# Low parts of twelve weight units made by TensorE and ScalarE in the bank that VectorE wrote, with the planner's numbers anew

## The chip, the cores and the metric

The kernel runs on one core of one Trainium2 chip. The metric is the device time of one execution in microseconds (us). An execution was timed three times before the change: 676.77, 675.38 and 676.64 us, median 676.64 us.

## What is computed

An attention over 4 batches of 8 heads, 576 tokens and 64 dimensions (causal, with a bias from a running sum of `s`), then two feed-forward layers over the 2304 tokens. Cut to what matters:

```
scores = q @ k^T / 8 ; causal ; + min(-(cum_i - cum_j), 0)      # cum = cumsum(max(s, 0))
attn   = exp(scores - max) / (sum + 1e-9) ; x = attn @ v         # (2304, 512)
h  = x @ w_in                                                    # 512 -> 1024
sm = softmax(h) ; solu = h * sm ; ln = normalise(solu) * g_ln
x  = ln @ w_out                                                  # 1024 -> 512
h  = max(x @ w1, x @ w2, x @ w3)                                 # 512 -> 768
out = h @ w_out2                                                 # 768 -> 512
```

Each product is made to nearly 32 bits out of three fp16 products: both operands are split into a high part (fp16 of the scaled value) and a low part (fp16 of what the high part leaves), and high by high, high by low and low by high are added up.

## The kernel before, in words

**Tiles and groups.** Tokens go through in 18 tiles of 128: per pair of batches eight full tiles and one of the two 64-token tails. A tile's attention is `sc` (scores on TensorE, L788 and L794), a masked minimum on VectorE (L825, L858), the exponential on ScalarE (L877), a split of its result into high and low part, a transposition, and `av` (the product with the values, L942, L948, L961). For tiles 0 to 3 transpositions are made by TensorE in `turned` (L474); for all others by a DMA transpose (`et<-es`, tails also `ett<-est`). Then comes the first layer `m1` (L1034) with its softmax and normalisation (L1048 to L1096), and, for groups of two tiles, `m2` (L1131), `m3` (three products for the maximum, L1170, combined by L1189) and `m4` (L1204).

**Weights.** They arrive as 64-bit floats and are decoded on the chip in 40 units of 128 x 512 by `load_w`: a DMA into one of four stages (L594), three VectorE instructions that put the 32-bit value together (`dec1` L608, `dec2` L612, `dec3` L615, the last two into a bank of PSUM), `wh` on ScalarE, which writes the scaled high part (L620), and `wl` on VectorE, which writes scale times value minus high part (L622). Units 0 to 7 are `w_in`, 8 to 15 `w_out` (their scale is a column of `g_ln`), 16 to 33 `w1`, `w2`, `w3`, and 34 to 39 `w_out2`.

**Banks.** The bank of a unit is one of the three of the pool `acc`, which `turned`, `m2`, `m3` and `m4` take theirs from too. Scores, values and `h` have banks of their own.

**A low part by TensorE.** `turned` does already what the change will do for weights: after ScalarE or VectorE has written the high part, a matmul with a diagonal of -1/scale (`MINUS`, made at L532) adds minus the high part to the bank (L488), and a copy moves scale times the rest out (L491 or L492).

**Order.** No loop sets the order of instructions. `build` makes a list of operations, each with a position `pos` worked out from the table `P`, the engines that may take it and an estimate of its time; `Schedule.run` plays them through with a clock of its own, gives each engine among those that can start soon the one of lowest position, and issues everything in the order found. On the chip each engine then takes its instructions strictly in that order. A DMA counts in this plan as landed `LAT_DMA` ns after its share of the queue is over:

```
    LAT_SAME, LAT_CROSS, LAT_DMA, LAT_ISSUE = 130, 180, 1250, 650
```

Tiles of `et` (four buffers), `es` (two), `r` (three) and the three `acc` banks bound how far one engine may run ahead of another.

Of the kernel before, what the change touches and what calls it, by code (L numbers as in the profile page):

```python
# [18 lines left out]
QK_S = 16.0  # L19
# [14 lines left out]
    la=8.4,  # L34
    lp=-1.469,
    lu=-13.333,
    lv=-0.647,
    o1=-3.616,
    o2=-4.09,
    o3=-0.398,  # L40
    o4=0.334,
    ds=1.887,
    wi=-20.819,
    wid=2.708,
    wo=-15.551,
    wod=-18.167,
    w3=6.958,
    w3d=1.141,
    w4=-16.623,
    w4d=15.675,  # L50
    mp=-1.93,
    look=[2.7, 0.0, 35.7, 169.7, 69.9],
    spare=[1764.9, 1665.2, 1871.5, 968.8, -1500.0, 3960.7, 27.5],
# [6 lines left out]
    lc=-23.89,  # L60
# [35 lines left out]
class Schedule:  # L96
# [5 lines left out]
    def __init__(self, look, spare, off, eng):  # L102
        self.ops, self.last, self.readers = [], {}, {}
        self.look = dict(zip(("PE", "DVE", "ACT", "POOL", "SP"), look))

        self.spare = [dict(zip(("DVE", "ACT", "POOL"), spare[i:i + 3])) for i in (0, 3)]
        self.spare_until = spare[6]
        self.off, self.eng = off, eng
        self.unit, self.tile = "", ""

# [34 lines left out]
    def run(self):  # L145
# [114 lines left out]
        for _ in self.ops:  # L260
# [67 lines left out]
def pe(k, n):  # L328
    return k * (n / 2.4 + 2.3)
# [22 lines left out]
def build(nc, T, X, dims):  # L352
# [17 lines left out]
    S_ = Schedule(P["look"], P["spare"], P["off"], P["eng"])  # L370

# [91 lines left out]
    SCALES = (QK_S, -QK_S, E_S, 1.0)  # L463
    MINUS = lambda c: T["k_tail"][:, 2 + SCALES.index(c)]

    def turned(n, src, out, scale, r, w, pos, k):
# [11 lines left out]
        op([("PE", pe(n, 256) + 20, f)], r + ["ktail"], [ps], pos, kind=k + "p")  # L478
# [7 lines left out]
        if by_pe:  # L486
# [11 lines left out]
           [ps] + w[0], w[1], pos, kind="P" + k)  # L498

# [10 lines left out]
    def prologue():  # L510
# [8 lines left out]
        if any(P["pt"]):  # L519

            def ident():
                nc.gpsimd.memset(IDENT(), 1.0)
                for s in (1, -1):
                    nc.gpsimd.affine_select(
                        out=IDENT(), in_=IDENT(), pattern=[[-s, 128]], base=0, channel_multiplier=s,
                        compare_op=ALU.is_ge, fill=0.0,
                    )
            op([("POOL", 900, ident)], [], ["ktail"], p0 - 1, kind="ident")

            def minus():  # L530
# [55 lines left out]
    def load_w(src, hi, lo, scale, pos, wkey, extra=()):  # L586
# [17 lines left out]
        pb = buf("acc")  # L604
        f32 = lambda: pb().rearrange("p (b n) -> p b n", b=8)
        i32 = lambda: pb().bitcast(I32).rearrange("p (b n) -> p b n", b=8)
        def dec1():
# [3 lines left out]
        op([("DVE", dve1(512), dec1)], sk, [tb], pos, kind="dec1")  # L611
        op([("DVE", dve2(512), lambda: nc.vector.scalar_tensor_tensor(  # L612
            out=i32(), in0=low(), scalar=29, in1=t(), op0=ALU.logical_shift_right, op1=ALU.bitwise_or))],
           sk + [tb], [pb], pos, kind="dec2")
# [6 lines left out]
           [pb] + list(extra), [(wkey, 0)], pos, kind="wh")  # L621
        op([("DVE", dve2(512) + px * 0.57, lambda: nc.vector.scalar_tensor_tensor(  # L622
# [529 lines left out]
    def m3(g, f0):  # L1152
# [11 lines left out]
        for w in range(3):  # L1164
            ps, first = buf("acc"), ([], [])
            for f in (f0, f0 + 1):
                for kk in range(KD):
# [6 lines left out]
                    o = op([("PE", pe(3, GN), fn)], [(xk[0], 0, kk), (xk[1], 1, kk), (("w3", f, w), 0), (("w3", f, w), 1)],  # L1174
# [192 lines left out]
```

## Time and profile before

| | |
|---|---|
| median of three runs | 676.64 us |
| profiled execution, its time | 676.31 us |
| its span, first to last instruction | 674.6 us |
| TensorE busy | 621.2 us (92%) |
| VectorE busy | 464.3 us (69%) |
| ScalarE busy | 301.8 us (45%) |
| mean granted TensorE clock | 0.994 |

The span is the trace's own; 1.7 us of the profiled execution's time lie around it. Shares of busy time are means over a program with different stretches: weights are decoded in the first quarter, attention runs to about 460 us, and from there TensorE works through the second layers alone.

### The profile page before, as it was taken

The numbers are of one execution on the slowest core, as the hardware profiler recorded it, in microseconds if no ns is written. First come the engines' busy times: TensorE is split into PE (matmuls) and PEld (weight loads), VectorE is DVE, ScalarE is ACT, GpSimd is POOL, SyncE is SP. The second block draws the span as 40 slices with busy tenths as digits, with TensorE's granted clock in tenths as the row PEclk, the third lists the DMA queues.
The fourth block names the chain that finished last, engine by engine and source line by source line (L and its number), as shares of the span: only waits on it lengthen the run. The fifth ranks groups of instructions, "written<-read, shape, count | busy, mean of one in ns | idle before, by whom it ended". The sixth has DMA issues, their size and how long they took to land.

```text
span 674.6 us, 15275 instructions
## 1 busy us (share of the span) xinstructions
PE 621.2 (92%) x6188; PEld 442.7 (66%) x6188; DVE 464.3 (69%) x1109; ACT 301.8 (45%) x713; POOL 34.1 (5%) x49
## 2 busy tenths in 40 slices
PE   1579888899999999899999999989999999999997
PEld 1334556777576666667666675659767867878774
DVE  7899999997799678798888988775155245212121
ACT  3678875554476445667556546351023022110110
POOL 1101000010001101020000201000000000000000
PEclk9998999999999999999999999989999999999999
DMA  6976755569989879699999896864032022000001
GB/s 176 276 216 176 171 153 162 172 144 186 170 167 176 155 142 150 131 186 189 162 181 174 152 181 119 127 99 84 1 63 63 1 48 48 1 32 2 17 17 32
DMA packets 249351, 82.68 MB, mean 123 GB/s; under 512 B 225472, under 2 KB 244096, under 8 KB 249280
## 3 DMA queue, kind: packets, MB, share of 16 engines
q1 hardware_dynamic: 249280, 81.70, 60.0%
q8 instruction: 48, 0.79, 0.5%
q14 instruction: 23, 0.19, 0.1%
HBM read 35.95 MB, written 4.83 MB: 60 GB/s over the span
## 4 chain that ended last, share of the span: by engine, by line
PE 63%; DVE 15%; DMA 14%; issue 3%; ACT 3%; SPq 1%; POOL 0%; DVEq 0%; POOLq 0%; ACTq 0%
PE acc L1170 23%; PE acc L1131 11%; PE acc L1204 9%; PE h L1034 8%; DMA et<-es 7%; PE sc L794 4%; PE av L961 3%; PE sc L788 2%; DVE acc L612 2%; DVE acc L615 2%; DVE r L825 1%; DMA kt<-in_moe_w_in_dram 1%; DMA vs<-in_moe_w_in_dram 1%; DVE f L608 1%; DMA lnt<-ln 1%
## 5 line engine op out<-in xcount | busy, mean ns | idle before, releaser
L1170 PE MATMUL acc<-x2A,w_h 128*128 128x256 f16 x1296 | 215.5, 273 | 2.3 <-DVE f L1189 1.5
L1170 PEld LDWEIGHTS <-w_h 128*128 128x128 f16 x1944 | 187.3, 98 | 32.6 <-issue 7.6
L1170 PE MATMUL acc<-x2B,w_h 128*128 128x256 f16 x648 | 176.7, 273 | 0.0
L877 ACT ACTIVATE r<-r,mn 128x128 f32<-128x128 f32 (+4 forms) x144 | 83.0, 578 | 55.0 <-DVE mn L825 39.7
L1034 PE MATMUL h<-w_in_h,xt 128*128 128x512 f16 x432 | 101.3, 380 | 0.0
L1131 PE MATMUL acc<-lnt,w_out_h 128*128 128x256 f16 x864 | 98.2, 273 | 1.1 <-DMA lnt<-ln 1.0
L1131 PEld LDWEIGHTS <-w_out_h 128*128 128x128 f16 x864 | 83.4, 98 | 13.3 <-issue 3.3
L1189 DVE TENSOR_TENSOR f<-f,acc 128x512 f32<-128x512 f32 x54 | 36.9, 684 | 69.8 <-PE acc L1170 69.8
L1034 PEld LDWEIGHTS <-xt 128*128 128x128 f16 x432 | 40.0, 98 | 45.7 <-issue 3.6
L454 ACT ACTIVATE f<-acc 128x512 f32<-128x512 f32 x37 | 22.0, 595 | 98.5 <-PE acc L1170 57.9
L1204 PE MATMUL acc<-w2o_h,h2A 128*128 128x512 f16 x216 | 64.4, 380 | 0.0
L825 DVE CUSTOM_DVE_ANT_0 r<-sc,mask 128x128 f32<-128x128 f32 (+3 forms) x128 | 58.7, 485 | 7.1 <-PE sc L794 5.5
L434 DVE SCALAR_TENSOR_TENSOR es<-r,es 128x512 f16<-128x512 f32 (+1 forms) x89 | 56.7, 642 | 2.3 <-ACT es L405 1.7
L794 PE MATMUL sc<-kt,qt 64*128 64x256 f16 (+2 forms) x768 | 47.9, 264 | 0.7 <-DMA kt<-st 0.4
L961 PE MATMUL av<-vs,et 128*128 128x64 f16 x960 | 38.1, 195 | 5.1 <-DMA et<-es 4.8
L961 PEld LDWEIGHTS <-et 128*128 128x128 f16 x960 | 34.9, 99 | 12.0 <-DMA et<-es 7.7
L405 ACT ACTIVATE es<-r 128x512 f16<-128x512 f32 (+1 forms) x48 | 28.0, 584 | 29.4 <-DMA et<-es 25.5
L1204 PE MATMUL acc<-w2o_h,h2B 128*128 128x512 f16 x108 | 41.0, 379 | 0.0
L1055 ACT ACTIVATE ln<-e,st 128x1024 f32<-128x1024 f32 x18 | 20.7, 1150 | 42.4 <-DVE e L1048 35.7
L788 PE MATMUL sc<-ckr,cqr 6*128 6x128 bf16 (+5 forms) x192 | 28.6, 308 | 11.9 <-DMA cqr<-cum_d 9.8
L794 PEld LDWEIGHTS <-qt 64*128 64x128 f16 (+1 forms) x864 | 26.8, 99 | 18.3 <-issue 11.2
L454 ACT ACTIVATE x2A<-acc 128x512 f16<-128x512 f32 x16 | 9.5, 593 | 64.0 <-PE acc L1131 64.0
(138 smaller groups left out, 721.3 us busy)
## 6 DMA issues: line engine op xcount, KB each, us to landing
kt<-in_moe_w_dram SPq DMA_DIRECT2D x18, 256.0 KB
vs<-in_moe_w_dram SPq DMA_DIRECT2D x18, 256.0 KB
raw<-in_k_dram SPq DMA_DIRECT2D x16, 256.0 KB
raw<-in_q_dram SPq DMA_DIRECT2D x16, 256.0 KB
raw<-in_v_dram SPq DMA_DIRECT2D x16, 256.0 KB
out_dram<-f SPq DMA_DIRECT2D x16, 256.0 KB
kt<-in_moe_w_out_dram SPq DMA_DIRECT2D x7, 512.0 KB
vs<-in_moe_w_out_dram SPq DMA_DIRECT2D x7, 512.0 KB
```

The costliest lines, as they stand in the source:

```text
L434: nc.vector.scalar_tensor_tensor(out=lo(g), in0=src(g), scalar=sc1(g), in1=hi(g), op0=ALU.mult, op1=ALU.subtract)
L454: nc.scalar.activation(out=out(*a), in_=in_(*a), func=AF.Copy, scale=scale)
L788: yield lambda: nc.tensor.matmul(out=out(), lhsT=T["cqr"][cr, hp, cs], rhs=T["ckr"][cr, hp, ck], start=True, stop=False, skip_group_check= ...
L794: yield lambda n=n, qa=qa, o=o, kx=kx: nc.tensor.matmul(out=out()[:, o], lhsT=qv()[r, qa * HP + hp, ts], rhs=kx, start=False, stop=(n == 2 ...
L825: nc.vector.tensor_tensor_reduce(out=gw(R)[:, g], in0=gw(sc[y])[:, g], in1=T["mask"][:, SM - W:SM], scale=1.0 / S_MUL, scalar=3e38, op0=AL ...
L877: nc.scalar.activation(out=gw()[:, g], in_=gw()[:, g], func=AF.Exp, bias=mnf()[:, g:g + 1], scale=-1.0, accum_out=den(hs[g]),)
L961: nc.tensor.matmul(out=out, lhsT=ea_[:, ea, kb], rhs=T["v_s"][c, kb // 2][:, kb % 2, ha + a, va], start=(kb == 0 and m == 0), stop=(kb == ...
L1034: nc.tensor.matmul(out=hb()[:, n * 512:(n + 1) * 512], lhsT=xt()[:, xa, kk], rhs=T["w_in_h"][:, wa, kk, n * 512:(n + 1) * 512], start=(kk ...
L1131: nc.tensor.matmul(out=ps()[:, d % 2 * GN:(d % 2 + 1) * GN], lhsT=T["w_out_h"][:, wa, kk, d * 128:(d + 1) * 128], rhs=lnt()[:, la, kk], st ...
L1170: nc.tensor.matmul(out=ps()[:, f % 2 * GN:(f % 2 + 1) * GN], lhsT=T["w123_h"][:, w, wa, f, kk], rhs=x2(xa)[:, kk], start=(kk == 0 and i == ...
L1189: op([("DVE", dve2(2 * GN), lambda ps=ps: nc.vector.tensor_tensor(out=m(), in0=m(), in1=ps(), op=ALU.max))], pk + [m], [m], pos, kind="m3x")
L1204: nc.tensor.matmul(out=ps(), lhsT=h2(ha)[:, f, o * 128:(o + 1) * 128], rhs=T["w2o_h"][:, wa, f], start=(f == 0 and i == 0), stop=(f == KF2 ...
```

## The change

Three things. For the units 0 to 19 whose scale is a plain number, that is the eight of `w_in` and four of `w1` to `w3`, VectorE's `wl` is replaced by a matmul `wm` with the diagonal of -1/256 that takes the high part off in the bank, and by a ScalarE copy `Pw` of the rest. For this the three `acc` banks are each written once by a matmul at the start (`prime_all`), since the first value in a unit's bank comes from VectorE and the matmul has to add to it; VectorE's second decode step waits for that, and so does the first transposition. `MINUS` gets a fifth column. Second, every `m3` matmul now also waits for the low part of the odd unit of its pair. Third, 19 numbers of the table `P` and two of its lists are new (two lines shown), and `LAT_DMA` is 2087 instead of 1250 ns, so the order of nearly everything changes.

```diff
 P = dict(
-    la=8.4,
+    la=7.39,
...
+    lat=2.087,
+    wp=[0, 20, 20],
...
+    S_.LAT_DMA = int(P["lat"] * 1000)
...
-    SCALES = (QK_S, -QK_S, E_S, 1.0)
+    SCALES = (QK_S, -QK_S, E_S, 1.0, W_S)
...
-        op([("PE", pe(n, 256) + 20, f)], r + ["ktail"], [ps], pos, kind=k + "p")
+        op([("PE", pe(n, 256) + 20, f)], r + ["ktail", "prime"], [ps], pos, kind=k + "p")
...
+    def prime(bank):
+
+        nc.tensor.matmul(
+            out=bank, lhsT=MINUS(1.0), rhs=T["k_tail"].rearrange("p h t -> p (h t)")[:, 0:512], start=True, stop=True,
+        )
...
+            def prime_all():
+                for b in T["acc"]:
+                    prime(b)
+            op([("PE", 700, prime_all)], ["ktail"], ["prime"], p0 - 1, kind="prime")
...
+        by_pe = not callable(scale) and P["wp"][0] <= n_w[0] - 1 < P["wp"][1]
...
-           sk + [tb], [pb], pos, kind="dec2")
+           sk + [tb, "prime"], [pb], pos, kind="dec2")
...
+        if by_pe:
+
+            op([("PE", pe(1, 512) + 60, lambda: nc.tensor.matmul(
+                out=f32(), lhsT=MINUS(scale), rhs=hi, start=False, stop=True, skip_group_check=True))],
+               ["ktail", (wkey, 0)], [pb], pos, kind="wm")
+            op([("ACT", act(512, True), lambda: nc.scalar.activation(out=lo, in_=f32(), func=AF.Copy, scale=scale))],
+               [pb], [(wkey, 1)], pos, kind="Pw")
+            return
...
-                    o = op([("PE", pe(3, GN), fn)], [(xk[0], 0, kk), (xk[1], 1, kk), (("w3", f, w), 0), (("w3", f, w), 1)],
+                    o = op([("PE", pe(3, GN), fn)], [(xk[0], 0, kk), (xk[1], 1, kk), (("w3", f, w), 0), (("w3", f, w), 1), (("w3", f0 + 1, w), 1)],
```

Three places of the order show what moves. In the kernel after the change the lines are numbered anew: `dec1` L634, `dec2` L640, `dec3` L643, `wh` L648, `wm` L652, `Pw` L655, the transposition L485, its subtraction L499, scores L824, m2 L1167, values of a tail L978.

VectorE's queue, first weight units, before: `f` is the scratch tile of `dec1`, `kt` and `vs` are the stages, `acc` the banks.

```order
L608 TENSOR_SCALAR f_114<-kt_69 128x512
L612 SCALAR_TENSOR_TENSOR acc_131<-kt_69,f_114 128x512
L608 TENSOR_SCALAR f_115<-vs_73 128x512
L615 SCALAR_TENSOR_TENSOR acc_131<-kt_69,acc_131 128x512
L612 SCALAR_TENSOR_TENSOR acc_129<-vs_73,f_115 128x512
L615 SCALAR_TENSOR_TENSOR acc_129<-vs_73,acc_129 128x512
L622 SCALAR_TENSOR_TENSOR w_in_h<-acc_131,w_in_h 128x512
L622 SCALAR_TENSOR_TENSOR w_in_h<-acc_129,w_in_h 128x512
L608 TENSOR_SCALAR f_116<-kt_69 128x512
L612 SCALAR_TENSOR_TENSOR acc_130<-kt_69,f_116 128x512
```

The same stretch of VectorE's queue after the change:

```order
L634 TENSOR_SCALAR f_114<-kt_69 128x512
L640 SCALAR_TENSOR_TENSOR acc_131<-kt_69,f_114 128x512
L643 SCALAR_TENSOR_TENSOR acc_131<-kt_69,acc_131 128x512
L634 TENSOR_SCALAR f_115<-vs_73 128x512
L640 SCALAR_TENSOR_TENSOR acc_129<-vs_73,f_115 128x512
L643 SCALAR_TENSOR_TENSOR acc_129<-vs_73,acc_129 128x512
L634 TENSOR_SCALAR f_116<-kt_69 128x512
L640 SCALAR_TENSOR_TENSOR acc_130<-kt_69,f_116 128x512
```

The two instructions that wrote low parts are gone, and the third unit stands right behind the second.

TensorE's queue at the program's start, before: the first transpositions of `k` and `q`, their subtractions, then the scores of tile 0.

```order
L474 MATMUL acc_129<-k_tail,raw_84 128x128 x4
L474 MATMUL acc_130<-k_tail,raw_85 128x128 x4
L488 LDWEIGHTS k_tail
L488 MATMUL acc_129<-kt_68,k_tail 128x512
L488 LDWEIGHTS k_tail
L488 MATMUL acc_130<-qt_88,k_tail 128x512
L788 LDWEIGHTS cqr
L788 MATMUL sc_125<-ckr,cqr 128x128
```

TensorE's queue there after the change (the three matmuls of `prime_all`, L513, stand ahead of these rows):

```order
L485 MATMUL acc_129<-k_tail,raw_84 128x128 x4
L485 MATMUL acc_130<-k_tail,raw_85 128x128 x4
L499 LDWEIGHTS k_tail
L499 MATMUL acc_129<-kt_68,k_tail 128x512
L499 LDWEIGHTS k_tail
L499 MATMUL acc_130<-qt_88,k_tail 128x512
L652 LDWEIGHTS k_tail
L652 MATMUL acc_131<-w_in_h,k_tail 128x512
L652 LDWEIGHTS k_tail
L652 MATMUL acc_129<-w_in_h,k_tail 128x512
L652 LDWEIGHTS k_tail
L652 MATMUL acc_130<-w_in_h,k_tail 128x512
```

The subtractions of the first three weight units now stand ahead of the scores of tile 0.

TensorE's queue in the last tail tile (17), at the start of the value products of its second pair of heads, before: the last rows of a score tile (`sc`), three matmuls of `m4`, then the value products (`av<-v_tail,ett`).

```order
L794 LDWEIGHTS qt_89
L794 MATMUL sc_126<-kt_70,qt_89 64x256
L1204 LDWEIGHTS h2A_112
L1204 MATMUL acc_131<-w2o_h,h2A_112 128x512
L1204 LDWEIGHTS h2A_112
L1204 MATMUL acc_131<-w2o_h,h2A_112 128x512
L1204 LDWEIGHTS h2B_113
L1204 MATMUL acc_131<-w2o_h,h2B_113 128x512
L942 LDWEIGHTS ett_102
L942 MATMUL av_127<-v_tail,ett_102 128x64
```

The same value products after the change:

```order
L1167 LDWEIGHTS w_out_h
L1167 MATMUL acc_130<-lnt_108,w_out_h 128x256
L1167 LDWEIGHTS w_out_h
L1167 MATMUL acc_130<-lnt_108,w_out_h 128x256
L1167 LDWEIGHTS w_out_h
L1167 MATMUL acc_130<-lnt_108,w_out_h 128x256
L978 LDWEIGHTS ett_101
L978 MATMUL av_127<-v_tail,ett_101 128x64
```

What stands between a pair's scores and its values is other work now, and more of it: here 33 matmuls of `m2` stand right ahead where three of `m4` stood. In the order of instructions VectorE has 1069 rows where it had 1086, ScalarE 513 where it had 495 and TensorE 12184 where it had 12154.

## Rows read from the trace of the kernel before

**Rows 1.** Busy time, share of the span and instructions of each engine.

```profile
PE 621.2 (92%) x6188; PEld 442.7 (66%) x6188; DVE 464.3 (69%) x1109; ACT 301.8 (45%) x713; POOL 34.1 (5%) x49
```

**Rows 2.** Stretches: length, busy us of each engine (instructions), granted clock, DMA share, GB/s.

```profile
0.00:20.00 20.00, 6.02 (x42) 3.18 (x42) 15.76 (x28) 6.25 (x10) 3.26 (x12) 1.00 0.70 190
20.00:112.00 92.00, 72.57 (x576) 44.03 (x577) 86.96 (x222) 68.64 (x171) 5.77 (x7) 0.98 0.72 194
112.00:140.00 28.00, 25.40 (x224) 21.68 (x222) 27.53 (x54) 13.83 (x27) 0.00 (x0) 1.00 0.55 168
140.00:460.00 320.00, 307.26 (x3656) 212.22 (x3656) 267.01 (x691) 180.80 (x440) 25.05 (x30) 0.99 0.89 156
```

**Rows 3.** TensorE's waits, 0 to 112 us: for whom, us, times, longest.

```profile
PE sc L788 <- DMA cqr<-cum_d: 8.8, 1, 8.8
PE acc L474 <- DVE w_in_h L622: 5.7, 1, 5.7
PE acc L488 <- ACT qt L481: 3.3, 3, 2.6
```

**Rows 4.** Timeline of VectorE, weight units 2 to 4: start, us, instruction [idle before].

```profile
14.72 0.43 DVE L608 TENSOR_SCALAR f<-kt 128x512 int32<-128x512 int32 x1 [1.32 <-DMA kt<-in_moe_w_in_dram]
...
17.32 0.43 DVE L608 TENSOR_SCALAR f<-vs 128x512 int32<-128x512 int32 x1 [0.64 <-DMA vs<-in_moe_w_in_dram]
...
20.30 0.43 DVE L608 TENSOR_SCALAR f<-kt 128x512 int32<-128x512 int32 x1 [0.56 <-DMA kt<-in_moe_w_in_dram]
```

**Rows 5.** Groups by line and form: count, busy us, mean ns, idle before.

```profile
L622 DVE SCALAR_TENSOR_TENSOR w_in_h<-acc,w_in_h 128x512 f16<-128x512 f32 x8 | 5.4, 684 | 0.7 <-ACT w_in_h L620 0.6
L491 ACT ACTIVATE et<-acc 128x512 f16<-128x512 f32 x9 | 5.3, 605 | 1.0 <-PE acc L488 1.0
```

**Rows 6.** Timeline of VectorE at 82 us, one instruction behind the other.

```profile
82.03 0.69 DVE L612 SCALAR_TENSOR_TENSOR acc<-vs,f 128x512 int32<-128x512 int32 x1
82.64 0.68 DVE L492 TENSOR_SCALAR et<-acc 128x512 f16<-128x512 f32 x1
```

**Rows 7.** Timeline of TensorE: the first transposition of exponentials, subtractions, the first m3.

```profile
25.69 1.94 PE L474 MATMUL acc<-k_tail,r 128*128 128x128 f32 x8 [5.71 <-DVE w_in_h L622]
27.46 0.60 PE L488 MATMUL acc<-et,k_tail 128*128 128x512 f16 x1
...
51.17 0.38 PE L488 MATMUL acc<-qt,k_tail 128*128 128x512 f16 x1 [2.58 <-ACT qt L481]
...
77.56 0.66 PE L474 MATMUL acc<-k_tail,r 128*128 128x128 f32 x4 [0.27 <-DVE lnt L492]
...
111.58 0.38 PE L1170 MATMUL acc<-x2A,w_h 128*128 128x256 f16 x2 [0.60 <-ACT lnt L491]
```

**Rows 8.** The chain that ended last, dense stretch: start, us, what.

```profile
464.34 9.82 PE acc L1170 x90
...
484.65 5.18 PE h L1034 x24
```

**Rows 9.** TensorE's waits, 112 to 470 us.

```profile
PE av L961 <- DMA et<-es: 4.8, 9, 1.0
PE av L942 <- DMA ett<-est: 3.3, 2, 2.0
```

**Rows 10.** Timeline of TensorE, last tail tile: end of a pair's scores, its values.

```profile
436.75 0.20 PE L794 MATMUL sc<-k_tail,qt 64*64 64x64 f16 x4
...
448.51 0.29 PE L942 MATMUL av<-v_tail,ett 128*128 128x64 f16 x2 [2.00 <-DMA ett<-est]
```

**Rows 11.** Chain in that stretch: a transpose, from issue to landing.

```profile
430.67 4.61 DMA et<-es
```

**Rows 12.** Stretches with a lower granted clock (columns as in Rows 2).

```profile
52.00:54.00 2.00, 1.85 (x14) 0.86 (x13) 2.00 (x5) 0.87 (x2) 0.00 (x0) 0.55 0.67 103
...
448.00:450.00 2.00, 1.49 (x28) 1.49 (x29) 1.74 (x6) 0.00 (x0) 0.00 (x0) 0.54 0.84 160
450.00:452.00 2.00, 2.00 (x40) 1.76 (x41) 1.60 (x3) 1.61 (x3) 0.00 (x0) 0.61 1.01 195
```

More of the change, by code (lines that the diff above doesn't have):

```diff
@@ L33 @@
 P = dict(
-    la=8.4,
[L35 to L53, printed above, removed]
+    la=7.39,
+    lp=-0.608,
+    lu=-16.19,
+    lv=-1.406,
+    o1=-3.612,
+    o2=-4.645,
+    o3=-0.487,
+    o4=-0.249,
+    ds=1.922,
+    wi=-17.837,
+    wid=2.329,
+    wo=-18.404,
+    wod=-17.549,
+    w3=7.111,
+    w3d=1.066,
+    w4=-19.979,
+    w4d=18.0,
+    mp=-3.058,
+    look=[0.0, 0.0, 0.0, 174.5, 0.0],
+    spare=[1764.9, 1665.2, 1805.0, 80.4, -1500.0, 3810.9, 28.4],
     n_st=4,
@@ L59 @@
     nr=3,
-    lc=-23.89,
+    lat=2.087,
+    wp=[0, 20, 20],
+    lc=-23.622,
     S=[],
@@ L109, in __init__ @@
         self.unit, self.tile = "", ""
+        self.primed = []
     def op(self, alts, reads, writes, pos, dma=0, kind="", mode=""):
@@ L321, in run @@
                     add(s)
+        for b in self.primed:
+            for x in b.pool.bufs:
+                if x.slot == b.slot and x.users[0].kind in ("m2", "m3") and min(u.start for u in x.users) < min(u.start for u in b.users):
+                    raise RuntimeError("not marked")
         out.sort(key=lambda o: (o.start, o.index))
@@ L604, in load_w @@
         pb = buf("acc")
+        by_pe = not callable(scale) and P["wp"][0] <= n_w[0] - 1 < P["wp"][1]
+        if by_pe:
+            if n_w[0] <= P["wp"][2]:
+                S_.primed.append(pb)
         f32 = lambda: pb().rearrange("p (b n) -> p b n", b=8)
@@ L611, in load_w @@
         op([("DVE", dve1(512), dec1)], sk, [tb], pos, kind="dec1")
+        if by_pe and n_w[0] > P["wp"][2]:
+            op([("PE", pe(1, 512) + 20, lambda: prime(pb()))], ["ktail", tb], [pb], pos, kind="wz")
         op([("DVE", dve2(512), lambda: nc.vector.scalar_tensor_tensor(
             out=i32(), in0=low(), scalar=29, in1=t(), op0=ALU.logical_shift_right, op1=ALU.bitwise_or))],
-           sk + [tb], [pb], pos, kind="dec2")
+           sk + [tb, "prime"], [pb], pos, kind="dec2")
         op([("DVE", dve2(512), lambda: nc.vector.scalar_tensor_tensor(
@@ L621, in load_w @@
            [pb] + list(extra), [(wkey, 0)], pos, kind="wh")
+        if by_pe:
+            op([("PE", pe(1, 512) + 60, lambda: nc.tensor.matmul(
[4 more added lines that the diff above has]
+            return
         op([("DVE", dve2(512) + px * 0.57, lambda: nc.vector.scalar_tensor_tensor(
```

## The prediction, made before the changed kernel ran

> **What bounds the kernel now.** I read the busy table first [rows 1]: TensorE is busy for 621 of 674.6 us, so the end can only move if its waits shrink or its work changes. The table by stretches [rows 2] says where the waits are. From 0 to 112 us TensorE is idle for 14.0 and 19.4 us while VectorE is busy for 87.0 of 92 us from 20 us on: there VectorE sets the pace. From 112 to 140 us the first m3 products run, with 2.6 us of idle TensorE. From 140 to 460 us TensorE is idle for 12.7 us of 320. Third, TensorE's waits: early ones are for the running sum's DMA (8.8 us), for VectorE's `wl` that holds a bank (5.7 us) and for ScalarE's high parts [rows 3]; later ones are mostly for DMA transposes of the exponentials, 4.8 and 3.3 us [rows 9]. So there are two places to win, VectorE's queue before the first m3, and the distance between scores and values after it. The profiled execution took 676.3 us, its span 674.6, and 1.7 us lie around it; it is 0.3 us under the median of 676.6, so a sum against it needs no correction.
>
> **Removed from VectorE.** Twelve `wl` at 0.684 us [rows 5]. One behind the other, such instructions start 0.61 us apart [rows 6], so 12 x 0.61 = 7.3 us of VectorE's queue go. The planner also hands VectorE other work. I counted VectorE's queue up to the second low part of x2 (the last thing that group 0's m3 needs of x2): 233 instructions before, 220 after. The difference is 13 fewer `wl`, one weight unit fewer, one low part of `v` fewer, and a net four more copies of transposed tiles; each instruction at its group's mean of the trace, that is 8.5 us less in a queue of 111.6 us. Durations overlap (0.69 long, 0.61 apart [rows 6]), so in time it is 8.5 x 0.88 = 7.5 us.
>
> Not all of it counts. VectorE waits for the DMA of units 2, 3 and 4 anyway, 1.32 + 0.64 + 0.56 = 2.5 us [rows 4], and their DMAs start little earlier: the first stage comes free by about 0.5 us sooner, since `dec3` of unit 0 no longer stands behind `dec1` of unit 1. The four `wl` taken out ahead of 20.3 us (2.4 us) therefore only lengthen these waits. Left are 7.5 - 2.5 = **5.0 us** by which the first m3 starts sooner than 111.58 us [rows 7]. Bounds: 0 (another engine takes over the pace) and 8.7 us (a later mark, VectorE's first maximum in m3, lies 10.0 us earlier in its queue, times 0.88 in time).
>
> **Added to ScalarE.** Twelve `Pw`, for which the nearest row is the same copy of a transposed tile, 0.605 us [rows 5]: 7.3 us. Up to the second high part of x2, ScalarE's queue gets only 4.3 us longer (74.8 to 79.0 us), as VectorE took over copies. ScalarE is busy for 68.6 of 92 us there [rows 2], so there is room on the average, and I cost the time itself at nothing; without that cover it is 4.3 us.
>
> A rule speaks against this part: by the Trainium skill, "ScalarE: Activation LUTs", Rules for kernel authors, multiplies and adds belong on VectorE, which it puts at up to about three times ScalarE's rate per element on 16-bit data. Here the copy out of a bank takes 0.605 us on ScalarE against 0.684 us for VectorE's instruction [rows 5], so the trace does not bear it out for 32-bit values in PSUM. If it held, each `wl` removed would free only a third of ScalarE's 0.605 us, the front's term would be an estimated 1.5 us instead of 5.0, and the time 670.5 us; by the rows it stays.
>
> **Added to TensorE.** 15 matmuls of 512 columns, all ahead of the first m3. A subtraction took 0.60 us early on and 0.38 us later [rows 7]; back to back 512 columns take 5.18/24 = 0.216 us [rows 8]. So 3.2 us at least and 9 us at most, in a stretch in which TensorE idles for 33 us [rows 2]; the three at the start stand ahead of an 8.8 us wait for the running sum. Cost of the work: 0. But TensorE takes its queue in order: each `wm` waits for ScalarE's `wh`, and behind it wait transpositions, scores and m1. The rows nearest to it are the subtractions that waited for ScalarE, 3.3 us in 3 waits [rows 3]. If each of the 12 waited for 1.1 us on the path it were 13 us; if none, 0. Most find TensorE idle anyway, so I take **+1.0 us**. Against it, the bank that TensorE waited 5.7 us for [rows 3] now comes free through ScalarE before the first exponentials; but both transpositions of that tile use one bank in turn after the change, so I count no gain there.
>
> **Moved past the first m3.** Eight transpositions and two subtractions of tile 2's normalised rows stand ahead of m3 before, in or behind it after: 8 x 0.66/4 [rows 7] + 2 x 0.216 = **+1.7 us** of work behind that mark.
>
> **The first m3 itself.** Its idle is 2.6 us in 28 [rows 2], for weights and maxima from VectorE. VectorE's first maximum gains another 1.2 us on the first m3 (8.7 against 7.5). The new wait for the odd unit's low part reaches at most 12 matmuls x 0.109 us (9.82/90 [rows 8]) = 1.3 us further ahead than before, at the start of a pair. I take **-1.0 us**, between +1.3 and -2.6.
>
> **Attention after 140 us.** Here the new order does the work, not the low parts. In the last tail tile a pair's scores were done at 436.95 us, its values began at 448.51 us, and the last 2.0 us of this TensorE waited for a transpose [rows 10], so 11.6 us were needed. Between the two stood, beside scores and values, 21 matmuls of 512 columns: 21 x 0.216 = 4.5 us. After the change there are 117 of 256 columns, 117 x 0.109 = 12.8 us [rows 8], plus one more score part. That is over 8 us more cover for a wait of 2 us. Counted so for all 56 pairs of heads in tiles 4 to 17, the work between scores and values grows for 36, shrinks for 8 (of which seven keep at least 13 us), and stays for 12. A transpose takes 4.61 us from issue to landing [rows 11]; the old plan allows 0.65 + 0.90 + 1.25 us and the time of the issue (0.63), 3.4 us, the new one 4.3 us. This is why the new order leaves more room, and the trace sides with it. TensorE's waits for transposes are 8.1 us [rows 9]. After two waits its granted clock fell to about half (0.55 and 0.54 [rows 12], nearly the 1.2 GHz level); before either it had stood idle for 2.58 and 2.00 us [rows 7, 10]. The later fall lost 2 x 0.46 + 2 x 0.39 = 1.7 us [rows 12], and I take as much for the earlier one, which lies in front and is not counted there. Gain between 0 and 8.1 + 1.7 = 9.8 us here; new waits could eat into it, since four `et` buffers hold two pairs and a longer distance keeps them full (2 us the other way at worst, as long as the longest wait now). I take **-6.0 us**, somewhat over half, since 36 of 56 pairs gain cover and the pair with the longest wait gains most.
>
> **Sum.** -5.0 + 1.0 + 1.7 - 1.0 - 6.0 = -9.3 us: 676.3 - 9.3 = **667.0 us**, 1.4% less.
>
> **Rivals.**
>
> *The distance buys nothing.* With four `et` buffers, the transposes of the next pair but one cannot start until these values are done; a longer distance then only moves the wait to ScalarE and VectorE and comes back. For it: these buffers are as many as before. Against: in the tail, 8 us of work stand between the release of a buffer and its next use. Without the -6.0: 673.0 us.
>
> *ScalarE sets the pace in front.* It gets 4.3 us more, in order, mixed with waits for `wm`. For it: 75% busy [rows 2]. Against: before, it waits itself for VectorE. The front gains 0 instead of 5.0: 672.0 us.
>
> *Banks (the slower side).* A unit's bank was given back by `wl`; now it is held for `wm` (0.38 to 0.60 us) and `Pw` (0.605) instead of 0.684, two hand-overs between engines more, and a stay in TensorE's queue. TensorE's 5.7 us wait [rows 3] shows that banks bind. If each of the 12 units holds its bank for 1.5 us longer, that is 18 us on three banks, 6 us of the front. From about 3 us per unit on (12 us) it takes more than the whole change brings. With 6 us in front and half of the later gain: 676.3 + 6.0 + 1.7 - 1.0 - 3.0 = 680.0 us. Against it: the planner lays out banks itself and tile by tile finds other work.
>
> **Chances.** Forecast 0.57 (its own range 662 to 671), no use of the distance 0.15, ScalarE 0.08, banks 0.14, and 0.06 for partial gains and losses that cancel. A measurement of this kernel can tell 0.2% (1.4 us) from no change. Forecast and the first two rivals are faster, 0.80; the last case the same, 0.06; banks slower, 0.14. The range 660.5 to 677.5 takes in everything but most of the banks and little of the far end of the gain (front 8.7, attention 9.8: 660 us).
>
> **What would show it.** VectorE's first m3 maximum and the first m3 on TensorE about 5 us sooner (106 to 107 us); VectorE still over 93% busy from 20 us to there; waits of `wm` for `wh` of some 1 us in total that matter; TensorE's idle time from 140 us to the end of attention down from 12.7 to about 8 us, waits for `et` and `ett` under 4 us and no fall of the clock in the last tail; the stretch after attention as dense as before. I am wrong in the front if ScalarE is over 90% busy there or TensorE's waits for `wh` exceed 5 us, and wrong on the order if waits for transposes stay near 8 us.

## The result, and the profile after

The kernel after took 665.45 us (median of four runs, 664.21 to 667.48), the kernel before 676.7 us in runs beside it: a ratio of 0.9839, 95% interval 0.9811 to 0.9868. The profiled execution took 665.51 us, its span is 663.8 us, 10.8 us shorter than before.

Busy time of the kernel after, to set beside [rows 1]:

```profile
PE 622.2 (94%) x6203; PEld 443.8 (67%) x6203; DVE 454.0 (68%) x1093; ACT 309.5 (47%) x731; POOL 32.9 (5%) x49
```

TensorE is busy 1.0 us longer than before and the span is 10.8 us shorter, so 11.8 us of its idle time are gone. The stretches of [rows 2], after (same columns), say where:

```profile
0.00:20.00 20.00, 8.32 (x48) 3.99 (x49) 14.19 (x26) 8.31 (x13) 3.26 (x12) 0.80 0.68 188
20.00:112.00 92.00, 76.92 (x601) 46.33 (x600) 84.43 (x215) 69.11 (x174) 7.95 (x8) 0.90 0.72 192
112.00:140.00 28.00, 22.98 (x200) 19.27 (x197) 27.76 (x55) 15.07 (x29) 0.00 (x0) 1.00 0.57 176
140.00:460.00 320.00, 314.79 (x3623) 221.84 (x3622) 261.63 (x673) 180.52 (x442) 21.71 (x29) 1.00 0.88 154
```

Length minus TensorE's busy time: up to 112 us it idles for 26.8 us instead of 33.4, from 112 to 140 us for 5.0 instead of 2.6, from 140 to 460 us for 5.2 instead of 12.7. The first m3 (timeline of TensorE, as in [rows 7]) is 4.3 us sooner than 111.58 us:

```profile
107.32 0.38 PE L1206 MATMUL acc<-x2A,w_h 128*128 128x256 f16 x2
```

Yet both kernels end group 0's m3 and start tile 4's scores at 140.0 us. In these two profiles, what was won in front is given back in the m3 stage. The last matmul ends at 659.2 us instead of 670.0, so all of the 10.8 us fall behind 140 us. TensorE's waits after, 107 to 140 us (for whom, us, times, longest):

```profile
PE acc L1206 <- DVE f L1225: 3.0, 3, 1.1
PE acc L1206 <- ACT f L465: 2.8, 2, 1.5
PE acc L485 <- DVE f L1225: 0.8, 1, 0.8
```

and its waits from 112 to 470 us, to set beside [rows 9]:

```profile
PE av L997 <- DMA et<-es: 2.4, 3, 1.2
...
PE h L1070 <- DMA xt<-xs: 0.8, 1, 0.8
```

The waits for the `et` transposes have halved (a third row, 0.3 us, goes with the first) and those for `ett` are gone. In the last tail tile (timeline of TensorE, as in [rows 10]) the second pair's scores are done at 451.0 us and its values begin at 468.78 us, 17.8 us later instead of 11.6, without a wait:

```profile
450.83 0.20 PE L830 MATMUL sc<-k_tail,qt 64*64 64x64 f16 x4
...
468.78 0.22 PE L978 MATMUL av<-v_tail,ett 128*128 128x64 f16 x2
```

TensorE's waits after, 0 to 112 us, where [rows 3] stood before:

```profile
PE acc L652 <- ACT w_in_h L648: 7.4, 3, 3.3
PE acc L513 <- DVE k_tail L549: 4.0, 1, 4.0
PE acc L499 <- DVE et L495: 2.7, 3, 2.1
PE acc L485 <- ACT r L913: 2.4, 1, 2.4
```

The waits for `cqr` (8.8 us) and for `wl` (5.7 us) have left, and `wm` waiting for `wh` has come. The groups of the new instructions (count, busy us, mean ns, idle before):

```profile
L655 ACT ACTIVATE w_in_h<-acc 128x512 f16<-128x512 f32 x8 | 4.7, 593 | 2.6 <-PE acc L652 2.5
L652 PE MATMUL acc<-w_in_h,k_tail 128*128 128x512 f16 x8 | 4.1, 513 | 7.5 <-ACT w_in_h L648 7.4
L655 ACT ACTIVATE w_h<-acc 128x512 f16<-128x512 f32 x4 | 2.2, 601 | 0.0
...
L652 PE MATMUL acc<-w_h,k_tail 128*128 128x512 f16 x4 | 1.4, 378 | 0.4 <-ACT w_h L648 0.4
```

VectorE's waits after, 0 to 140 us. All but 0.26 us of the two rows is the wait of units 2 to 4, the stretch of [rows 4]: 1.94 + 0.67 + 1.63 = 4.2 us, where it had been 2.5 us:

```profile
DVE f L634 <- DMA kt<-in_moe_w_in_dram: 3.8, 3, 1.9
...
DVE f L634 <- DMA vs<-in_moe_w_in_dram: 0.7, 1, 0.7
```

### The profile page after: what moved, and what is told of

The parts are those of the page before. It is cut to its first block, busy times and chain, and to the rows that moved or that the text cites. A ratio compares the mean times of both kernels' runs of the same rounds, so it can differ in the third digit from the quotient of the medians.

```text
span 663.8 us, 15326 instructions
## 1 busy us (share of the span) xinstructions
PE 622.2 (94%) x6203; PEld 443.8 (67%) x6203; DVE 454.0 (68%) x1093; ACT 309.5 (47%) x731; POOL 32.9 (5%) x49
## 4 chain that ended last, share of the span: by engine, by line
PE 68%; DVE 16%; DMA 8%; ACT 3%; issue 2%; SPq 1%; DVEq 0%; ACTq 0%
PE acc L1206 26%; PE acc L1167 11%; PE h L1070 10%; PE acc L1240 9%; PE sc L830 5%; PE av L997 3%; DMA et<-es 3%; DVE acc L640 3%; PE sc L824 2%; DMA kt<-in_moe_w_in_dram 2%; DVE acc L643 2%; DVE es L445 1%; DMA kt<-in_moe_w_dram 1%; DVE f L634 1%; PE acc L485 1%
## 5 line engine op out<-in xcount | busy, mean ns | idle before, releaser
L1206 PE MATMUL acc<-x2A,w_h 128*128 128x256 f16 x1296 | 215.8, 273 | 5.7 <-DVE f L1225 3.0
L1206 PEld LDWEIGHTS <-w_h 128*128 128x128 f16 x1944 | 187.4, 98 | 35.4 <-issue 9.6
L1206 PE MATMUL acc<-x2B,w_h 128*128 128x256 f16 x648 | 176.6, 273 | 0.0
L1167 PE MATMUL acc<-lnt,w_out_h 128*128 128x256 f16 x864 | 97.7, 273 | 0.0
L1167 PEld LDWEIGHTS <-w_out_h 128*128 128x128 f16 x864 | 83.5, 98 | 11.2 <-issue 1.0
L465 ACT ACTIVATE f<-acc 128x512 f32<-128x512 f32 x42 | 24.9, 593 | 94.7 <-PE acc L1240 58.2
L861 DVE CUSTOM_DVE_ANT_0 r<-sc,mask 128x128 f32<-128x128 f32 (+3 forms) x128 | 58.6, 486 | 10.8 <-PE sc L830 8.5
L997 PE MATMUL av<-vs,et 128*128 128x64 f16 x960 | 36.4, 194 | 2.5 <-DMA et<-es 2.4
L416 ACT ACTIVATE es<-r 128x512 f16<-128x512 f32 (+1 forms) x45 | 26.0, 580 | 23.6 <-DMA et<-es 18.8
L1240 PEld LDWEIGHTS <-h2A 128*128 128x128 f16 x216 | 20.5, 98 | 21.6 <-issue 0.8
L1084 DVE TENSOR_SCALAR_CACHE_REDUCE e<-h 128x1024 f32<-128x1024 f32 x18 | 21.9, 1219 | 18.9 <-PE h L1070 18.5
```

The lines of the kernel that those rows point to most:

```text
L416: eng.activation(out=out(g), in_=src(g), func=AF.Copy, scale=sc(g))
L465: nc.scalar.activation(out=out(*a), in_=in_(*a), func=AF.Copy, scale=scale)
L861: nc.vector.tensor_tensor_reduce(out=gw(R)[:, g], in0=gw(sc[y])[:, g], in1=T["mask"][:, SM - W:SM], scale=1.0 / S_MUL, scalar=3e38, op0=AL ...
L997: nc.tensor.matmul(out=out, lhsT=ea_[:, ea, kb], rhs=T["v_s"][c, kb // 2][:, kb % 2, ha + a, va], start=(kb == 0 and m == 0), stop=(kb == ...
L1167: nc.tensor.matmul(out=ps()[:, d % 2 * GN:(d % 2 + 1) * GN], lhsT=T["w_out_h"][:, wa, kk, d * 128:(d + 1) * 128], rhs=lnt()[:, la, kk], st ...
L1206: nc.tensor.matmul(out=ps()[:, f % 2 * GN:(f % 2 + 1) * GN], lhsT=T["w123_h"][:, w, wa, f, kk], rhs=x2(xa)[:, kk], start=(kk == 0 and i == ...
```

## The experiments

Each ratio is to the kernel before, run on the same chip in the same minutes, with a 95% interval. Where an expectation speaks of a time, the ratio is what to read: in these runs the kernel before took 677.7 to 678.4 us.

**The change in parts (e1 to e4, e11).** Theory: the order makes the gain. Rival: the low parts make it. e1 is the kernel after with the table and latency of before:

```diff
-    la=7.39,
+    la=8.4,
...
-    lat=2.087,
+    lat=1.25,
```

> The kernel before with the twelve low parts by TensorE and ScalarE, but with its old table and the old 1250 ns for a DMA's landing (the planner orders anew around the new steps). Theory 'order' (the time came from the distance between scores and values after 140 us; the low parts' gain before the first m3 is given back while VectorE paces m3): the first m3 starts 3 to 5 us sooner than at 111.6 us, the waits of values for transposes stay near 8 us, and the time is 673 to 678 us. Rival 'low parts' (the relief of VectorE is what counts): 667 to 670 us.

Ratio 0.9950 (0.9925 to 0.9975), in the theory's range. Two of its steps missed: with all twelve low parts off VectorE the first m3 came at 112.3 us and not 3 to 5 us sooner than 111.6, and TensorE's waits for transposes were 2.8 us and not near 8. e2 is the kernel after with all low parts on VectorE:

```diff
-    wp=[0, 20, 20],
+    wp=[0, 0, 0],
```

> The changed kernel with its new table and 2087 ns, but with all low parts by VectorE as before (the banks are still written once at the start). Theory 'order': most of the gain is there, 665 to 669 us, TensorE idle from 140 to 460 us under 7 us, the first m3 not sooner than 110 us. Rival 'low parts': 673 to 677 us.

Ratio 0.9924 (0.9898 to 0.9951), between the two: the theory's 665 to 669 us are ratios of 0.983 to 0.989, the rival's 673 to 677 us 0.995 to 1.000. Its first m3 came at 104.89 us, against the theory, sooner than in the kernel after and with no relief for VectorE at all. Its time was lost later, in a wait of TensorE (112 to 470 us) for the masked minimum `mn`, of which the kernel after has 0.4 us:

```profile
PE sc L824 <- DVE mn L861: 6.7, 3, 4.5
```

e3 is the kernel before with the new latency alone:

```diff
-    LAT_SAME, LAT_CROSS, LAT_DMA, LAT_ISSUE = 130, 180, 1250, 650
+    LAT_SAME, LAT_CROSS, LAT_DMA, LAT_ISSUE = 130, 180, 2087, 650
```

> The kernel before with one number changed: a DMA is taken to land 2087 instead of 1250 ns after its share of the queue. The mean work between scores and values of tiles 4 to 17 hardly grows by the order (14.3 to 14.6 us), with some pairs as low as 8 us. Theory 'the latency number makes the distance': 667 to 671 us. Rival 'table and latency only together': 674 to 679 us, since tile 7 now has 8 to 10 us where it had 16 to 18.

Ratio 0.9971 (0.9945 to 0.9998), as the rival had it, although waits for transposes fell to 2.8 us here too. e4 is the kernel after with the old latency (`lat=1.25`, one line):

> The changed kernel with 1250 instead of 2087 ns in the plan, all else as changed. The mean work between scores and values falls from 16.1 to 14.2 us by the order, as before the change (14.3). Theory 'order': waits for transposes come back, 8 us or more, and the time is 671 to 676 us. Rival 'low parts': 665 to 668 us.

Ratio 1.0009 (0.9982 to 1.0036). The whole gain is gone, which neither expectation had, although its first m3 is the soonest of all, 103.72 us. The waits for transposes are back, 8.9 us in all, as the theory had it. Its waits from 112 to 470 us:

```profile
PE av L997 <- DMA et<-es: 6.7, 11, 1.4
PE acc L1206 <- DVE f L1225: 5.3, 3, 3.2
PE sc L830 <- DMA kt<-st: 2.4, 1, 2.4
PE av L978 <- DMA ett<-est: 2.2, 4, 1.0
```

e11 is e1 with the new latency (`lat=2.087`):

> Low parts by TensorE and ScalarE and the planned latency of 2087 ns, but the old table of positions. Theory (latency and low parts are worth 0.3% and 0.5% alone, and add up; the table gives the rest): ratio 0.990 to 0.994, TensorE idle after 140 us 7 to 10 us. Rival (the latency number is what makes the order, the table is worth little): ratio 0.983 to 0.987, as the kernel after, idle after 140 us 4 to 6 us.

Ratio 0.9875 (0.9837 to 0.9913), between the theory's 0.990 to 0.994 and the rival's 0.983 to 0.987, with an interval that reaches both; the idle time, 7.1 us, is the theory's. The parts do not add up: the same low parts go with 0.9950, 0.9875, 1.0009 or 0.9839, depending on table and latency, which act on the chip through the order alone.

**The distance in the last tail (e5, e6).** e5 is the kernel before with tile 17's transposes planned later, e6 the kernel after with them planned sooner (there 600 for 2600); ahead of tile 17 nothing moves:

```diff
-                o.end = dma + self.LAT_DMA
+                o.end = dma + (2600 if o.kind[:2] == "eT" and o.cls[-3:] == "@17" else self.LAT_DMA)
```

> The kernel before, with one planned number changed: the DMA transposes of tile 17's exponentials alone count as landed 2600 ns late instead of 1250, so that the planner puts two or three more blocks of TensorE work between scores and values in that one tile (10 to 11 us of work become 12 to 13); everything ahead of tile 17 keeps its order. Distance theory (more TensorE work between a pair's scores and its values takes the wait for the transposes away, and with it the fall of the clock): the 2.0 us wait for ett in [rows 10] goes, the clock does not fall behind it, 2.5 to 4 us less, ratio 0.994 to 0.996. Rival (distance buys nothing, the wait moves on to another instruction): within 1 us of the kernel before, ratio 0.9985 to 1.0015, TensorE idle in 400 to 460 us as before.

Ratio 0.9930 (0.9906 to 0.9954). TensorE's stretch from 400 to 460 us, where the kernel before was busy for 56.14 us at a clock of 0.97:

```profile
400.00:460.00 60.00, 59.05 (x837) 40.37 (x836) 49.95 (x136) 31.38 (x74) 2.45 (x4) 1.00 0.78 127
```

2.9 us of idle time are gone by one number for one tile, and TensorE waits for no `ett` there any more. The pair of [rows 10] again has 11.6 us between scores and values, all of it work now. The theory holds, with a ratio just below its 0.994 to 0.996. The fall of the clock in [rows 12] is gone too, but it need not follow from the wait: in e9 (below), which keeps the order of the kernel before, the same values waited as long and the granted clock stayed at 1.00 (timeline of TensorE; the stretch of the last row of [rows 12]):

```profile
449.67 0.23 PE L944 MATMUL av<-v_tail,ett 128*128 128x64 f16 x2 [2.05 <-DMA ett<-est]
```

```profile
450.00:452.00 2.00, 2.00 (x75) 1.80 (x75) 2.00 (x6) 0.47 (x1) 0.00 (x0) 1.00 1.04 196
```

> The kernel after, with tile 17's transposes planned as landed 600 ns after the queue instead of 2087: the work between scores and values in that one tile shrinks from 21, 20, 15 and 13 us to 11, 11, 9 and 8 us, everything ahead of tile 17 keeps its order. Distance theory: waits for ett and et of 2 us or more are back and the clock falls behind one of them, 3 to 5 us more than the kernel after (ratio to the kernel before 0.988 to 0.992). Rival (distance buys nothing): the same as the kernel after within 1 us (ratio 0.983 to 0.985).

Ratio 0.9841 (0.9811 to 0.9870): no loss, so here the theory missed. One pair waited (timeline of TensorE):

```profile
448.54 0.20 PE L830 MATMUL sc<-k_tail,qt 64*64 64x64 f16 x4
...
454.91 0.20 PE L830 MATMUL sc<-k_tail,qt 64*64 64x64 f16 x4
...
460.16 0.23 PE L978 MATMUL av<-v_tail,ett 128*128 128x64 f16 x2 [0.88 <-DMA ett<-est]
...
464.35 0.22 PE L978 MATMUL av<-v_tail,ett 128*128 128x64 f16 x2
464.96 0.52 PE L984 MATMUL av<-vs,et 128*128 128x64 f16 x12 [0.39 <-DMA et<-es]
```

The pair whose scores ended at 448.7 us had 11.4 us and waited 0.88 us; the next, from 455.1 us on, had 9.2 us and did not wait for `ett`, and for `et` right behind it only 0.39 us. What a pair needs is not one figure. In this tile the kernel after had distance to spare, which was worth nothing.

**Low parts of the first units (e7, e12) and VectorE's work by itself (e9, e10).** e7 gives the first two units' low parts back to VectorE, e12 all eight of `w_in`:

```diff
-    wp=[0, 20, 20],
+    wp=[2, 20, 20],
```

> The kernel after, with the low parts of the first two weight units back on VectorE (two more instructions of 0.68 us ahead of 20 us, two matmuls and two ScalarE copies fewer; the rest of the order is the same). Step of the prediction: there VectorE waits for the DMA of the units anyway, so the two only fill these waits: first m3 within 0.4 us of the kernel after's 107.3 us and the time within 0.2% of it (ratio 0.982 to 0.986). Rival (every instruction off VectorE's queue counts in the front): 1.2 us later at the first m3, 1.2 us more time or up to 1.5 us.

Ratio 0.9836 (0.9796 to 0.9875), first m3 at 107.01 us: the two instructions cost nothing, as the prediction had it for those ahead of 20.3 us.

> The kernel after with only four of the twelve low parts made by TensorE and ScalarE (units 16 to 19); all eight of w_in are written by VectorE again, 8 x 0.68 = 5.5 us more in its queue; table, latency and the new m3 wait stay, and the planner orders anew (work between scores and values 9.5 us at least and 16.2 us on the mean over 56 pairs, against 7.9 and 16.1 in the kernel after). Theory (VectorE's relief in the front buys next to nothing, the order makes the gain): within 0.3% of the kernel after, ratio 0.981 to 0.987, TensorE idle after 140 us 4 to 7 us. Rival (the eight low parts of w_in carry the front's gain): first m3 4 to 5 us later than 107.3 us, group 0's m3 later by as much, ratio 0.989 to 0.993.

Ratio 0.9794 (0.9761 to 0.9828), no worse than the kernel after. The rival's time falls, although the first m3 comes 3.3 us later. It is no proof that the eight low parts are worth nothing: the planner ordered anew, and its order is better behind 140 us. First m3, the stretch after 140 us, and waits up to 140 us:

```profile
110.66 0.38 PE L1206 MATMUL acc<-x2A,w_h 128*128 128x256 f16 x2
```

```profile
140.00:460.00 320.00, 317.17 (x3632) 224.74 (x3630) 263.78 (x679) 171.78 (x424) 22.16 (x30) 1.00 0.90 152
```

```profile
PE sc L824 <- DMA cqr<-cum_d: 8.8, 2, 6.0
PE acc L485 <- DVE w_in_h L658: 5.5, 1, 5.5
```

TensorE's early waits are those of [rows 3] again, and it idles for 31.6 us up to 112 us (26.8 in the kernel after), but for 2.8 us only after 140 us. Group 0's m3 ends at 146.3 us; the new order had put scores of the next tiles in between, from 131.7 us on.

e9 keeps the order of the kernel before and only makes the twelve instructions shorter; e10 does so for fourteen others in the kernel after (`thin` is true for units 20 to 33 there):

```diff
-        op([("DVE", dve2(512) + px * 0.57, lambda: nc.vector.scalar_tensor_tensor(
+        thin = n_w[0] - 1 in (0, 1, 2, 3, 4, 5, 6, 7, 16, 17, 18, 19)
+        op([("DVE", dve2(512) + px * 0.57, lambda: nc.vector.tensor_scalar(
+            out=lo, in0=hi, scalar1=2.0 ** -12, scalar2=None, op0=ALU.mult) if thin else nc.vector.scalar_tensor_tensor(
             out=lo, in0=f32(), scalar=sc(0), in1=hi, op0=ALU.mult, op1=ALU.subtract))],
```

> The kernel before, with its order on every engine kept row for row; the twelve instructions that the change removes (low parts of units 0 to 7 and 16 to 19) become a scaling of the high part within SBUF, which is shorter (an estimated 0.2 to 0.43 us instead of 0.684; the low parts of these units are not the true ones) and no longer reads the bank. VectorE's relief alone, nothing added to TensorE or ScalarE, nothing reordered. Theory (VectorE's queue sets the pace up to the end of group 0's m3, and what the change gave back there it gave back through its new order): the first m3 is 2 to 4 us sooner than 111.6 us, group 0's m3 ends 2 to 4 us sooner than 140.0 us, ratio 0.994 to 0.997. Rival (the stretch of m3 has a pace of its own, by the weights' DMA or the banks, so the gain is given back there whatever the order): first m3 sooner by 2 to 4 us, end of group 0's m3 within 1 us of 140.0 us, ratio 0.998 to 1.001.

Ratio 0.9986 (0.9960 to 1.0013), and neither mark came sooner: group 0's m3 ends at 140.7 us and the first m3 is at

```profile
111.81 0.38 PE L1172 MATMUL acc<-x2A,w_h 128*128 128x256 f16 x2 [0.60 <-ACT lnt L491]
```

The two groups of the shorter instruction (count, busy us, mean ns):

```profile
L623 DVE TENSOR_SCALAR w_in_h<-w_in_h 128x512 f16<-128x512 f16 x8 | 3.2, 407 | 0.5 <-ACT w_in_h L620 0.5
L623 DVE TENSOR_SCALAR w_h<-w_h 128x512 f16<-128x512 f16 x4 | 1.1, 285 | 0.0
```

So 12 x 0.684 - 3.2 - 1.1 = 3.9 us left VectorE's queue, about 2.8 us of it behind 20.3 us. The end of the stage and the time are the rival's, but both expectations had the first m3 sooner, and there both fall: nothing was won and then given back, hardly anything was won at all. VectorE's own waits from 20.3 to 112 us say where the time went: for TensorE it waited 3.2 us instead of 0.5, for DMAs 3.5 instead of 2.5. Two reserves: in this profile the clock fell once more in front than before, which may hide up to 1.7 us, and the interval just reaches the 0.4% that 2.8 us would be.

> The kernel after, with its order on every engine kept row for row; the fourteen low parts of units 20 to 33 that VectorE still writes become the same shorter scaling within SBUF (low parts of these units not the true ones). Theory (VectorE's queue paces the m3 stage, where it is busy for 27.8 of 28 us): group 0's m3 ends 3 to 6 us sooner than 140.0 us and the time is 2 to 6 us less than the kernel after's (ratio 0.975 to 0.981 to the kernel before). Rival (another pace lies right behind, the weights' DMA or the banks): end of group 0's m3 within 1.5 us of 140.0 us, ratio 0.982 to 0.985, and VectorE idles more in that stretch.

Ratio 0.9784 (0.9744 to 0.9825): the theory's figure, with an interval that overlaps the kernel after's. Group 0's m3 ended at 138.3 us, between the two expectations. The group of the shorter instruction, the stretch, and TensorE's waits from 107 to 140 us:

```profile
L659 DVE TENSOR_SCALAR w_h<-w_h 128x512 f16<-128x512 f16 x14 | 4.0, 289 | 0.4 <-ACT w_h L648 0.2
```

```profile
112.00:140.00 28.00, 23.11 (x208) 19.24 (x207) 25.93 (x56) 15.62 (x30) 0.70 (x2) 1.00 0.52 163
```

```profile
PE acc L1208 <- DVE f L1227: 2.3, 3, 0.8
PE acc L1208 <- ACT f L465: 2.0, 2, 1.3
PE acc L485 <- DVE f L1227: 1.3, 2, 0.8
```

VectorE now idles for 2.1 us of 28 and TensorE waits for 5.6 us instead of 6.6. From first m3 to tile 4's scores it takes 31.2 us; the kernel after took 32.8, e6 and e7, with the same order there, 32.4 and 32.1. So 14 x (0.688 - 0.289) = 5.6 us off VectorE's queue brought about 1 us in this stage: here the rival is nearer. Whether the run gained more than that is inside its interval.

**All plain-scale units (e8).** One line, `wp=[0, 40, 20]`; each unit from 20 on needs a matmul of its own that writes its bank first.

> The kernel after, with all units of plain scale (also the remaining ones up to unit 39, w1 to w3 and w_out2) given to TensorE and ScalarE. Theory that VectorE sets the pace in the first m3 stage (its 27.8 us of 28 us busy there): group 0's m3 ends 2 to 4 us sooner than 140.0 us, VectorE's wait for the maximum shrinks, and the time is 0 to 3 us less than the kernel after's (ratio 0.979 to 0.984). Rival (TensorE pays: 20 more matmuls of 0.22 to 0.38 us, 4 to 8 us, in a stretch in which it is 82% busy or more, and banks are held longer): 2 to 6 us more (ratio 0.987 to 0.993).

Ratio 1.0551 (1.0520 to 1.0582), far beyond both. VectorE's waits, 107 to 180 us:

```profile
DVE f L1225 <- PE acc L1206: 12.9, 5, 5.0
DVE x2B L1184 <- ACT x2A L465: 8.0, 2, 4.5
DVE acc L640 <- PE acc L513: 6.7, 5, 3.0
```

VectorE stood still for banks that wait in TensorE's queue (L513 writes them first, L1206 is m3), and group 0's m3 ended at 161.7 us. This is a wait of the kind of the prediction's rival of the banks, at a size where it decides; but the first write by TensorE, which the twelve units don't need, and the order came with it, so the price of one hand-over can't be read from it.

## Why the prediction was right in its number, and where its steps were not

665.5 us against 667.0 us forecast, inside the range. Two errors nearly cancelled, and that is luck: the front, forecast at -3.3 us, brought nothing in this pair of profiles, and attention, forecast at -6.0 us, brought -10.8. Other profiles shift this by a little. Tile 4's scores start at 140.0, 140.7 and 141.2 us in three kernels with the order of before up to there (before, e9, e5), at 140.1, 139.1 and 138.6 us in three with the order of after (after, e7 but for two low parts, e6). On the mean 1.4 us are left of the front's gain, and as much less belongs to attention; since such marks differ by over 1 us within either three, this is a hint and no more.

*The pace in front: the step that failed.* VectorE stayed busy as I said, or nearly (92% from 20 us to the first m3, for over 93%). I read its 87.0 of 92 us before as "VectorE's queue sets the first m3", and took work off the queue as time off the mark. The mark came out nearly as forecast (-4.3 against -5.0 us), for another reason: e9 takes nearly half of the twelve instructions' time away with the order kept and moves it by +0.2 us, or at best 1.5 us sooner, were the extra fall of the clock taken off; e1 takes all of them away and has it 0.7 us later; e2 takes nothing away and has it 6.7 us sooner. It is the order that moves this mark; which engine sets the pace under a given order is not shown. And the mark is not the end of the stage: at 140.0 us nothing of the 4.3 us was left in this profile, and e4, with the soonest first m3 of all, gained nothing over the kernel before. The high busy share showed that VectorE had little slack, not that others waited for it; what I should have asked is which of TensorE's waits ended with VectorE: 10.7 of the 32.8 us that its waits from 0 to 112 us name, 5.7 us of them in the one wait of [rows 3].

*The first low parts only lengthen DMA waits.* Right: 2.5 us became 4.2 us for the same units, and e7 shows no cost for two of them.

*ScalarE's copies.* The price was right: 0.593 and 0.601 us for 0.605. That they are hidden is not shown. ScalarE is 75% busy from 20 to 112 us, under the 90% of my sign, but a busy share says as little of ScalarE as it did of VectorE. Of TensorE's waits from 0 to 112 us, 17.2 us end with ScalarE after the change and 8.4 us before (VectorE 9.0 and 10.7, DMAs none and 13.7), and the front brought next to nothing, as the rival that ScalarE sets the pace had it. e9 wins nothing either, with no copy added, so the rival is not needed to explain the front; but no run shortens ScalarE's copies with the order kept, and it stays open. The rule of the Trainium skill ("ScalarE: Activation LUTs", Rules for kernel authors) puts multiplies on VectorE as up to about three times faster per element in bf16; for 32-bit values in a bank, which that figure does not cover, these rows show no such gain: 0.59 to 0.60 us on ScalarE, against 0.68 us for VectorE's copy of the same size [rows 6]. No term hangs on it, and my estimate by it was not for this case.

*TensorE's added work.* 4.1 + 1.4 us for the twelve `wm` and 1.46 us for the first three, 7.0 us, within 3.2 to 9. I had said that waits for `wh` above 5 us would prove me wrong in the front; they are 7.8 us, and the front's term did fail. Yet the sign alone says little: e12 has no `wm` for `w_in`, and there `cqr` and `wl` hold TensorE for 14.3 us. I costed this work at nothing, and by the account of the two profiles it was not free: from 0 to 140 us TensorE idles for 31.8 us instead of 36.0 and is busy for 108.2 us instead of 104.0. The added 7.0 us, less the 2.1 us of the next paragraph, used up what the shorter idle time gave. No run tests this by itself.

*Moved past the first m3.* Right in kind: the transpositions and subtractions of one tile, 1.3 + 0.8 = 2.1 us for 1.7, lie behind 140 us now.

*The m3 stage, forecast -1.0, was +4.3 us.* TensorE waited 6.6 us there, for maxima from VectorE and copies from ScalarE by which its banks come free; before it waited 2.4 us. e10 shows that VectorE's weights are not the main cause; which hand-over is, stays open. The change's new wait of `m3` for the odd unit has no share: without that condition the planner writes the same program, byte for byte, so it binds nothing on the chip, and the bound of 1.3 us that I set for it was not needed.

*Attention: right in mechanism, mis-sized.* Forecast -6.0 us of at most 9.8, measured -10.8 with 2.1 us more work in it, so past my bound. Of the 10.8 us, idle time gave 12.7 - 5.2 = 7.5 and a shorter busy time 3.3. Waits for transposes fell from 8.4 to 2.7 us (forecast: under 4), and most of the small waits for `mn`, `cqr` and `lnt` went too. The clock did not fall in the last tail; I had tied the 1.7 us of that fall to the wait, and e9 shows that they are not tied. The same matmuls of scores and values took 125.6 us instead of 130.0, of which the fall explains a part; the rest I did not see coming, and it is not settled. e5 shows the mechanism in one tile, and e4 its reverse over all of them: one planned number, waits for transposes back at 8.9 us, and the gain gone. But short waits for transposes are not enough: e1, e2 and e3 have 2.4 to 2.8 us of them, as the kernel after, and gain 0.3 to 0.8%, since other waits of TensorE stand in their place. "The distance buys nothing" holds only where there is more of it than a pair needs (e6).

What orders the runs, but for the four from 9.3 to 9.9 us and small differences, is how long TensorE idles from 140 to 460 us (320 minus the busy time of that row). The last column is its waits there for transposes (`et` and `ett`):

| kernel | idle, us | ratio | first m3, us | for transposes, us |
|---|---|---|---|---|
| e8 | 24.5 | 1.0551 | 115.8 | 2.6 |
| e4 | 13.3 | 1.0009 | 103.7 | 8.9 |
| e9 | 12.8 | 0.9986 | 111.8 | 9.1 |
| before | 12.7 | 1 | 111.6 | 8.4 |
| e5 | 9.9 | 0.9930 | 112.7 | 6.1 |
| e2 | 9.8 | 0.9924 | 104.9 | 2.4 |
| e1 | 9.7 | 0.9950 | 112.3 | 2.8 |
| e3 | 9.3 | 0.9971 | 110.4 | 2.8 |
| e11 | 7.1 | 0.9875 | 108.4 | 3.2 |
| e7 | 5.2 | 0.9836 | 107.0 | 2.3 |
| after | 5.2 | 0.9839 | 107.3 | 2.7 |
| e6 | 5.1 | 0.9841 | 106.3 | 2.2 |
| e10 | 5.0 | 0.9784 | 107.2 | 2.6 |
| e12 | 2.8 | 0.9794 | 110.7 | 1.7 |

The first m3 orders nothing. So the low parts themselves are not shown to be worth time: under the order that the planner found for it, e12 does without eight of the twelve. Whether the four of units 16 to 19 are, or whether e12 and e2 differ (0.9794 and 0.9924) only by the order that the planner found around them, stays open. No version clearly beats the kernel after; e12 does with a third of its low parts what that does with twelve.

## What to carry to other kernels

A busy share near 95% on an engine with its own queue is no proof that it sets the pace: shorten some of its instructions with the order kept, and see whether the mark moves. Choose marks behind which nothing can be given back, here the idle time of the engine that is the bound. Where a planner writes the order, separate the edit from the new order before crediting either: here one planned latency for one tile was worth 0.7%, and the low parts under the old table and latency, with the order that came with them, 0.5%.

## What the runs showed of the hardware

The granted clock of the kernel before reads 1.00 from 20 to 34 us (0.98 for 20 to 112 us in [rows 2]), yet its matmuls of 512 columns took 0.58 us there, and 0.38 us from 33.92 us on. Timeline of TensorE, kernel before:

```profile
28.44 0.58 PE L488 MATMUL acc<-et,k_tail 128*128 128x512 f16 x1 [0.38 <-ACT et L481]
...
33.92 0.38 PE L488 MATMUL acc<-xt,k_tail 128*128 128x512 f16 x1
```

The kernel after has the same durations until 34 us, and there the record shows them (stretch, columns as above):

```profile
20.00:34.00 14.00, 8.39 (x48) 4.39 (x47) 11.53 (x36) 10.01 (x29) 0.89 (x1) 0.56 0.92 270
```

So both run near the 1.2 GHz level until about 34 us, and a mean clock of 0.979 against 0.994 says nothing of which ran slower; the durations of like matmuls do. In front the clock also falls at other places in runs with one and the same order: before at 52 to 56 us, in e5 at 51 to 62, in e9 at 45 to 49 and 76 to 80. Marks there are good to about 1 us: 107.3, 107.0, 106.3 and 107.2 us for the first m3 of four kernels whose order is the same up to it or nearly so (after, e7, e6, e10), and 111.6, 112.7 and 111.8 us for three with the order of before (before, e5, e9).
